# One decode step of attention and a gated MLP: VectorE's program becomes a loop, the head sum moves to TensorE, and the last w_out block is loaded by its own transfer

## The chip, the core and the metric

The kernel runs on one core of a Trainium2 chip. The core has TensorE (PE in the profile, with its weight loads as PEld), VectorE (DVE), ScalarE (ACT), GpSimd (POOL) and SyncE (SP), and 16 DMA engines that bring data from HBM. The time of a run is the device's, in microseconds. Three runs of the kernel before took 678.70, 678.88 and 678.92 us; the median is 678.88 us.

## The reference

Everything is in 32-bit floats. For a batch of 8 and one new position, with x of 512 features:

```python
xn = layernorm(x)
# attention over a cache of 4096 positions: 32 query heads, 8 key/value heads, head size 128
q = xn @ wq
scores = einsum("bhqd,bhkd->bhqk", q, k) * 128 ** -0.5
o = einsum("bhqk,bhkd->bhqd", softmax(scores), v)
s = o @ wo
# gated MLP: w_in is 512 x 1792, w_out is 896 x 512
z = gelu(xn @ w_in)
g = w_sp * layernorm(z[..., 896:]) + b_sp
y = (z[..., :896] * g) @ w_out
out = x + s * silu(y)
```

The caches are 134 MB each; wq and wo are 8.4 MB each, and w_in and w_out 5.5 MB together. Every byte is used once.

## The kernel before

**Slots.** Three SBUF buffers (`slot_A`, `slot_B`, `slot_C`) of 64 KB per partition take all loads, which SyncE issues in one order: wq into B, w_in with w_out into C, then for each of the eight key/value heads half of K into A, the other half into B, half of V into C, the other half into B. Each such half is 8 MB in 128 rows of 64 KB. SyncE waits before each load until TensorE has read the slot's previous content, so normally two loads are queued. In the last head V's first half goes into A, its second half comes in two parts of 4 MB, and wo comes into C: the first 12 of its 32 blocks ahead of V's second half (`load_wo(0, WO_EARLY)`), the rest behind it in six pieces that get smaller (`WO_LATE`: up to block 20, 25, 28, 30, 31, 32).

**Before the heads.** `project_q` makes the queries, `mlp` the gate. `mlp` ends in a product over w_out's seven blocks of 128 rows (L474), all of them columns of one transfer, `w_mlp`.

**A head** (`head`). `scores` (L506) multiplies the queries, spread out in `qz`, with K for four batch entries per slot. `softmax` takes maximum, exponent and sum over `sc`, and transposes the weights into `pT`. Then for each batch entry b: `values` (L538) forms eight products of 512 columns in `o_ps[b % 2]`. The wanted rows of this block are those where the row's group equals the column's; VectorE multiplies by the mask `diag` (L540) and adds over the groups (L541) to get `o_sb`; `combine` (L544) multiplies `o_sb` with `fold`, one product, into four columns of `po`. TensorE takes `combine(b - 1)` behind `values(b)`. I call `values` and the `combine` behind it a unit. After the last head, `folded_wo` (L566), `direct_wo` (L574) and a sum over groups (L625) multiply with wo; VectorE multiplies with the gate and adds x (L630, L631), and SyncE stores the result.

**What sets the order.** A `Recorder` collects every engine's instructions in the order in which the Python code names them, finds what each must wait for, and writes the programs. TensorE's program holds heads 0 to 6 as one loop, with waits on a semaphore `token` that is counted down by one each time, and the last head written out. VectorE's program before is written out from start to end, all eight heads.

Of the kernel before, what the change touches and what calls it, by code (L numbers as in the profile page):

```python
# [15 lines left out]
P = 128  # L16
# [24 lines left out]
BANK = 512  # L41

# [37 lines left out]
class Op:  # L80
    def __init__(self, eng, name, args, kw, line):
        self.eng, self.name, self.args, self.kw, self.line = eng, name, args, kw, line
        self.reads, self.writes = [], []
        self.waits = []
        self.sem = None
        self.iter = None
        self.pos = None


class Recorder:  # L90
# [6 lines left out]
    NAMES = ["tensor", "vector", "scalar", "gpsimd", "sync"]  # L97

    def __init__(self, nc):
# [4 lines left out]
        self.rounds = 0  # L104
        self.order = {n: [] for n in self.NAMES}
        self.dma_sems = {}
# [3 lines left out]
    @contextmanager  # L110
    def round(self, i):
        self.now = i
        self.rounds = max(self.rounds, i + 1)
        self.count = {n: 0 for n in self.NAMES}
        yield
        self.now = None

    def add(self, eng, name, args, kw):
# [3 lines left out]
        key = kw.pop("key", None)  # L122
# [15 lines left out]
        if self.now is not None:  # L138
            op.iter, op.pos = self.now, self.count[eng]
            self.count[eng] += 1  # L140
        op.at = len(self.order[eng])
# [3 lines left out]
        op.deps = set()  # L145
# [25 lines left out]
    def plan(self):  # L171
# [18 lines left out]
        body = [op for op in self.order["tensor"] if op.iter is not None]  # L190
        size = len(body) // self.rounds
        rounds = [body[i * size:(i + 1) * size] for i in range(self.rounds)]
        place = {(o.eng, o.iter, o.pos): o for o in self.ops if o.iter is not None}
        for p in range(size):
            need = set()
            for i, ops in enumerate(rounds):
                assert ops[p].pos == p and ops[p].name == ops[0 * size + p].name
                for o in ops[p].waits:
                    assert o.iter == i, (ops[p].line, ops[p].name, i, o.eng, o.line, o.iter)
                    need.add((o.eng, o.pos))  # L200
            for i, ops in enumerate(rounds):
                ops[p].waits = [place[e, i, q] for e, q in sorted(need)]
        takes = [o.pos for op in rounds[0] for o in op.waits if not o.dma]
        assert takes == sorted(set(takes)), takes
        assert all(o.dma or o.eng == "vector" for op in rounds[0] for o in op.waits)

        for op in self.ops:
            op.token = op.counted = False
        for op in self.ops:
            for o in op.waits:  # L210
                if o.dma:
                    continue
                if op.eng == "tensor" and op.iter is not None:
                    o.token = True
                else:
                    o.counted = True
        for p in range(size):
            any_ = any(ops[p].counted for ops in rounds)
            for ops in rounds:
                ops[p].counted = any_  # L220

        nc = self.nc
        self.first = None
        self.sems = {}

        def sem(name):
            if name not in self.sems:
                self.sems[name] = nc.alloc_semaphore(name)
            return self.sems[name]

        for n in self.NAMES:
            c = 0
            for op in self.order[n]:
                if op.dma:
                    op.sem = sem(op.key or f"dma{op.n}")
                    op.taken = op.key is not None
                    continue
                if op.token and op.counted:
                    c += 1
                elif op.counted:  # L240
                    c += 1
                op.level = c
            sem(n)
        sem("token")

    def emit_op(self, op):
        nc = self.nc
        eng = getattr(nc, op.eng)
        with nc.source_location(__file__, op.line, op.name):
            waits = []  # L250
            for o in sorted(op.waits, key=lambda o: o.n):
                if o.dma:
# [3 lines left out]
                    else:  # L256
                        waits.append((o.sem, 16))
                elif op.eng == "tensor" and op.iter is not None:
                    t = self.sems["token"]
                    eng.wait_ge(t, 1).then_inc(t, -1)  # L260
                else:
                    waits.append((self.sems[o.eng], o.level))
            for s, v in waits:
# [6 lines left out]
            elif op.counted:  # L270
                ins.then_inc(self.sems[op.eng], 1)
                if op.token:
                    eng.wait_ge(self.sems[op.eng], op.level).then_inc(self.sems["token"], 1)
            elif op.token:
                ins.then_inc(self.sems["token"], 1)

    def emit(self):
        nc = self.nc
        self.plan()
        for n in self.NAMES[1:]:  # L280
            for op in self.order[n]:
                self.emit_op(op)
        ops = self.order["tensor"]
        inside = [i for i, op in enumerate(ops) if op.iter is not None]
        size = len(inside) // self.rounds
        for op in ops[:inside[0]]:
            self.emit_op(op)
        with nc.tensor.Fori(0, self.rounds):
            for op in ops[inside[0]:inside[0] + size]:
                self.emit_op(op)  # L290
        for op in ops[inside[-1] + 1:]:
# [28 lines left out]
def gqa_gmlp_decode(real, x, kT, v, wq, wo, w_mlp, out):  # L320
# [13 lines left out]
    for c in range(0, XW, XW // X_PARTS):  # L334
# [22 lines left out]
    nc.vector.tensor_reduce(same[:, 0, :], ident.rearrange("p (g r) -> p r g", g=G),  # L357
                            op=ALU.add, axis=AX.X)
    for g in range(1, G):
        nc.vector.tensor_copy(same[:, g, :], same[:, 0, :])  # L360
    same_all = same.rearrange("p g r -> p (g r)")
    diag = sb("diag", [P, G])
# [302 lines left out]
```

## Time and profile before

| what | value |
|---|---|
| median of three runs | 678.88 us |
| span of the profiled execution, first to last instruction | 677.3 us |
| instructions profiled | 5857 |
| busy: PE, PEld, DVE, ACT | 375.2, 119.5, 167.5, 13.4 us |
| moved by DMA | 290.90 MB, mean 429 GB/s |
| result's store, issue to landing | 1.5 us |

The profile page gives the execution's span and no total of its own; the median lies 1.58 us above the span, for what stands around the first and the last instruction. "PEclk" in a window is the TensorE clock that the throttle granted, 1.00 or 0.50. "DMA share" is the busy share of the 16 DMA engines by the packets that start in a window, so short windows can go above 1. In a timeline row the columns are start, length, engine, line, operation, output and inputs, shape and count; the brackets hold the engine's idle time before it and what ended it. A product of 32-bit floats appears as two MATMUL and two LDWEIGHTS.

### The profile page before, as it was taken

The numbers are of one execution on the slowest core, as the hardware profiler recorded it, in microseconds if no ns is written. First come the engines' busy times: TensorE is split into PE (matmuls) and PEld (weight loads), VectorE is DVE, ScalarE is ACT, GpSimd is POOL, SyncE is SP. The second block draws the span as 40 slices with busy tenths as digits, with TensorE's granted clock in tenths as the row PEclk, the third lists the DMA queues.
The fourth block names the chain that finished last, engine by engine and source line by source line (L and its number), as shares of the span: only waits on it lengthen the run. The fifth ranks groups of instructions, "written<-read, shape, count | busy, mean of one in ns | idle before, by whom it ended". The sixth has DMA issues, their size and how long they took to land. (4 is left out here: it accounts for less than half of the span.)

```text
span 677.3 us, 5857 instructions
## 1 busy us (share of the span) xinstructions
PE 375.2 (55%) x2658; PEld 119.5 (18%) x2658; DVE 167.5 (25%) x277; ACT 13.4 (2%) x27; POOL 2.8 (0%) x14
## 2 busy tenths in 40 slices
PE   0547554546665455456755454655654465655657
PEld 0122121112111111111211121211211121111212
DVE  2141042302430033401521024401432024400342
ACT  0000000000000000000000000000000000000000
POOL 1000000000000000000000000000000000000000
PEclk9967666878767678877766678887676678766697
DMA  8999999999999999999999999999999999999997
GB/s 373 449 434 434 433 434 433 434 433 433 433 433 433 433 433 433 434 433 433 433 433 433 433 434 433 433 433 437 437 437 437 433 437 445 433 437 434 404 423 318
DMA packets 6233, 290.90 MB, mean 429 GB/s; under 512 B 832, under 2 KB 848, under 8 KB 1360
## 3 DMA queue, kind: packets, MB, share of 16 engines
q1 hardware_dynamic: 6192, 290.75, 99.3%
q8 instruction: 7, 0.11, 0.1%
q10 hardware_dynamic: 32, 0.02, 0.0%
q14 instruction: 2, 0.02, 0.0%
HBM read 290.74 MB, written 0.03 MB: 429 GB/s over the span
## 5 line engine op out<-in xcount | busy, mean ns | idle before, releaser
L506 PE MATMUL sc<-slot_B,qz 128*32 128x512 f32 x512 | 74.4, 746 | 76.6 <-PEq L506 76.6
L538 PE MATMUL o_ps<-slot_B,tbuf 128*16 128x512 f32 x512 | 77.5, 732 | 70.5 <-PEq L538 61.6
L506 PE MATMUL sc<-slot_A,qz 128*32 128x512 f32 x512 | 74.4, 746 | 47.6 <-PEq L506 47.6
L540 DVE TENSOR_TENSOR o_all<-o_ps,diag 128x512 f32<-128x512 f32 x64 | 44.3, 691 | 161.0 <-PE o_ps L538 161.0
L538 PE MATMUL o_ps<-slot_C,tbuf 128*16 128x512 f32 x448 | 67.0, 739 | 20.5 <-PEq L538 20.5
L510 DVE TENSOR_REDUCE nm<-sc 128x1 f32<-128x1024 f32 x8 | 9.8, 1224 | 269.5 <-PE sc L506 269.5
L541 DVE TENSOR_REDUCE o_sb<-o_all 128x128 f32<-128x512 f32 x64 | 67.8, 1060 | 2.2
L506 PEld LDWEIGHTS sc<-slot_B,qz 128*32 128x32 f32 x512 | 20.4, 134 | 130.5 <-issue 130.5
L506 PEld LDWEIGHTS sc<-slot_A,qz 128*32 128x32 f32 x512 | 20.7, 133 | 94.8 <-issue 94.8
L544 PE MATMUL po<-fold,o_sb 128*128 128x4 f32 x128 | 25.6, 270 | 12.3 <-PEq L544 12.3
L544 PEld LDWEIGHTS po<-fold,o_sb 128*128 128x128 f32 x128 | 20.3, 199 | 68.5 <-issue 64.2
L538 PEld LDWEIGHTS o_ps<-slot_B,tbuf 128*16 128x16 f32 x512 | 13.4, 106 | 100.5 <-issue 90.2
L538 PEld LDWEIGHTS o_ps<-slot_C,tbuf 128*16 128x16 f32 x448 | 13.7, 112 | 57.0 <-issue 56.8
L528 PE MATMUL scr<-ident,pbuf 128*128 128x128 f32 x64 | 14.8, 409 | 10.6 <-PEq L528 9.3
L511 ACT ACTIVATE pbuf<-sc,nm 128x1024 f32<-128x1024 f32 x8 | 8.9, 1114 | 556.1 <-DVE nm L510 556.1
L528 PEld LDWEIGHTS scr<-ident,pbuf 128*128 128x128 f32 x64 | 11.8, 211 | 11.0 <-issue 9.7
L529 DVE COPY tbuf<-scr 128x512 f32<-128x512 f32 x16 | 11.1, 692 | 10.6 <-PE scr L528 10.6
L415 PE MATMUL scr<-slot_B,xnT 128*32 128x512 f32 x64 | 9.0, 713 | 8.2 <-PEq L415 8.2
L538 PE MATMUL o_ps<-slot_A,tbuf 128*16 128x512 f32 x64 | 9.8, 753 | 3.9 <-PEq L538 3.9
L514 PE MATMUL scr<-ident,nm 128*1 128x128 f32 x8 | 2.2, 269 | 11.8 <-PEq L514 10.4
L394 PE MATMUL scr<-ident,tbuf 8*128 8x8 f32 x4 | 0.6, 255 | 12.9 <-DVE tbuf L391 12.9
L521 PE MATMUL scr<-wl,same 128*128 128x1 f32 x16 | 3.5, 286 | 6.1 <-PEq L521 5.4
(102 smaller groups left out, 88.4 us busy)
## 6 DMA issues: line engine op xcount, KB each, us to landing
slot_B<-in_v SPq DMA_DIRECT2D x2, 4096.0 KB, 33.8
slot_C<-in_w_mlp SPq DMA_DIRECT2D x1, 5376.0 KB, 34.2
slot_C<-in_wo SPq DMA_DIRECT2D x1, 3072.0 KB, 35.4
slot_C<-in_wo SPq DMA_DIRECT2D x1, 2048.0 KB, 41.4
slot_C<-in_wo SPq DMA_DIRECT2D x1, 1280.0 KB, 44.0
slot_C<-in_wo SPq DMA_DIRECT2D x1, 768.0 KB, 45.4
slot_C<-in_wo SPq DMA_DIRECT2D x1, 512.0 KB, 46.1
slot_C<-in_wo SPq DMA_DIRECT2D x2, 256.0 KB, 46.4
```

The source lines that it names most:

```text
L415: nc.tensor.matmul(pq[R * g:R * (g + 1), :], xnT[:, k, :], wq_sb[:, k, lo:lo + REP * DH], start=(k == 0), stop=(k == NK - 1))
L506: nc.tensor.matmul(sc[R * g:R * (g + 1), c, :], qz[:, b * R:(b + 1) * R], k_sb[:, i, c, g, :], start=(b == 0), stop=(b == B - 1))
L510: nc.vector.tensor_reduce(nm, sc, op=ALU.max, axis=AX.XY, negate=True)
L511: nc.scalar.activation(p.rearrange("p j s -> p (j s)"), sc.rearrange("p c s -> p (c s)"), AF.Exp, bias=nm, accum_out=l)
L514: nc.tensor.transpose(a, nm, ident)
L521: nc.tensor.matmul(tot, same_all, wl, start=True, stop=True)
L528: nc.tensor.transpose(t[:, j * P:(j + 1) * P], p[:, 4 * c + j, :], ident)
L529: nc.vector.tensor_copy(pT[:, :, 4 * c:4 * c + 4].rearrange("p b j (g r) -> p (j g) b r", g=G), t.rearrange("p (m b r) -> p m b r", b=B, r ...
L538: nc.tensor.matmul(of[R * c:R * c + G * REP, :], pT[:, b, j, :], v_unit[:, j], start=(j < G), stop=(j >= J - G))
L540: nc.vector.tensor_mul(o_all[b % 2], o, diag[:, :, None].to_broadcast([P, G, DH]))
L541: nc.vector.tensor_reduce(o_sb[b % 2], o_all[b % 2].rearrange("p g d -> p d g"), op=ALU.add, axis=AX.X)
L544: nc.tensor.matmul(po[:, b * REP:(b + 1) * REP], o_sb[b % 2], fold, start=True, stop=True)
```

## The change

**VectorE's program** is a loop over all eight heads, with an inner loop of four rounds of two batch entries. Waits between looped engines become countdown semaphores, one for each pair of engines. To make a head's VectorE part the same each time, work moves: evictions and copies to ScalarE and GpSimd (`po` to `oT`, the queries, the MLP's copies, `qz`), and building `same` to GpSimd. The softmax has fewer steps, and its eight transposes go into `sc` and come out in one copy.

**The sum over groups** leaves VectorE. VectorE only copies `o_ps` to `o_cp` (L616 in the new numbering), and `combine` (L620) is four products that add up in PSUM, one for each group, with the part of `same` that picks that group's rows.

**The last block of w_out** is no longer in `w_mlp`, whose rows are 2 KB shorter. It comes as `w_ext`, 32 rows of 8 KB read as eight groups of four (the array in memory has a fifth, unused row in each group, so that the groups stay apart); `mlp` multiplies it as four chunks of 32 rows, with four small transposes more.

TensorE's program at the end of the last head, before. The rows are the products in program order, with `o_sb` as weights in L544:

```order
L538 MATMUL o_ps<-slot_B,tbuf 16x512 x8
L544 MATMUL po<-fold,o_sb 128x4
L538 MATMUL o_ps<-slot_B,tbuf 16x512 x8
L544 MATMUL po<-fold,o_sb 128x4
L566 MATMUL sc<-slot_C,oT 8x512 x8
L544 MATMUL po<-fold,o_sb 128x4
L566 MATMUL sc<-slot_C,oT 8x512 x4
L574 MATMUL sc<-slot_C,oT_end 32x64 x40
L625 MATMUL sc<-pbuf,same 32x64 x8
L574 MATMUL sc<-slot_C,oT_end 32x64 x24
```

And after (`ob` holds both `o_ps` and `po`):

```order
L613 MATMUL ob<-slot_B,tbuf 16x512 x8
L620 MATMUL ob<-same,o_cp 128x4 x4
L613 MATMUL ob<-slot_B,tbuf 16x512 x8
L620 MATMUL ob<-same,o_cp 128x4 x4
L643 MATMUL sc<-slot_C,oT 8x512 x8
L620 MATMUL ob<-same,o_cp 128x4 x4
L643 MATMUL sc<-slot_C,oT 8x512 x4
L651 MATMUL sc<-slot_C,oT_end 32x64 x40
L702 MATMUL sc<-pbuf,same 32x64 x8
L651 MATMUL sc<-slot_C,oT_end 32x64 x24
```

The order is the same; each of the three single products of L544 has become four.

VectorE's program from the first head to its end, after. Before, these places held eight heads written out, 260 rows in all:

```order
L588 TENSOR_REDUCE nm<-sc 128x1
L593 TENSOR_REDUCE full<-scr 1x128
L596 TENSOR_TENSOR w<-scr,nm 128x1
L598 TENSOR_TENSOR wl<-w,l 128x1
L600 RECIPROCAL wl<-scr 128x1
L601 TENSOR_SCALAR pbuf<-pbuf,w,wl 128x1024
L605 COPY tbuf<-sc 128x32x8x4
L347 UNCONDITIONAL_BRANCH
L616 COPY o_cp<-ob 128x512 x2
L347 REGISTER_ALU
L347 COMPARE_AND_BRANCH
L344 REGISTER_ALU
```

A head's program is now seven instructions ahead of the inner loop and two copies (L616) in it, which four rounds repeat.

SyncE's program at its start, before:

```order
L338 DMA slot_B<-in_wq 128x16384
L341 DMA slot_C<-in_w_mlp 128x10752
L547 DMA slot_A<-in_kT 128x16384
L547 DMA slot_B<-in_kT 128x16384
L553 DMA slot_C<-in_v 128x16384
```

And after:

```order
L409 DMA slot_B<-in_wq 128x16384
L412 DMA slot_C<-in_w_mlp 128x10240
L417 DMA slot_C<-in_w_ext 32x1x2048
L624 DMA slot_A<-in_kT 128x16384
L624 DMA slot_B<-in_kT 128x16384
```

One transfer, `w_ext`, stands between w_mlp and the first half of K.

The core of the diff:

```diff
-        nc.vector.tensor_mul(o_all[b % 2], o, diag[:, :, None].to_broadcast([P, G, DH]))
-        nc.vector.tensor_reduce(o_sb[b % 2], o_all[b % 2].rearrange("p g d -> p d g"), op=ALU.add, axis=AX.X)
+        with nc.turn(b // 2, b % 2):
+            nc.vector.tensor_copy(o_cp[b % 2], o)
...
-        nc.tensor.matmul(po[:, b * REP:(b + 1) * REP], o_sb[b % 2], fold, start=True, stop=True)
+        for g in range(G):
+            nc.tensor.matmul(po[:, b * REP:(b + 1) * REP], o_cp[b % 2][:, g, :], fold[:, g, :],
+                             start=(g == 0), stop=(g == G - 1))
...
-        nc.vector.tensor_copy(to, po.rearrange("p (b r) -> p r b", r=REP))
+        nc.stored = nc.scalar.activation(to, po.rearrange("p (b r) -> p r b", r=REP), AF.Copy)
...
-        nc.vector.tensor_copy(qz.rearrange("p (b s) -> p b s", b=B)[:, :, :REP], qT[:, h])
+        nc.gpsimd.tensor_copy(qz.rearrange("p (b s) -> p b s", b=B)[:, :, :REP], qT[:, h], after=nc.stored)
...
+        with nc.vector.Fori(0, HKV):
+            for op in first:
+                if op is turn[0]:
+                    with nc.vector.Fori(0, count):
+                        for q in turn:
+                            self.emit_op(q)
+                elif op.turn is None:
+                    self.emit_op(op)
...
+XG, XR = 8, 4
+XK = XG * XR
+XC = P // XK
+LAST = NB - 1
...
-    n_in, n_mlp = NK * 2 * FH, NK * 2 * FH + NB * D
+    n_in, n_mlp = NK * 2 * FH, NK * 2 * FH + LAST * D
...
+    ext = slots["C"][:XK, n_mlp:n_mlp + XC * D]
+    nc.sync.dma_start(ext, w_ext[:, :XR])
+    w_ext_sb = ext.rearrange("p (c d) -> p c d", d=D)
...
-        for j in range(NB):
+        low = R * (LAST // 2)
+        hX = tbuf[:XK, 2 * P + D:2 * P + D + XC * R].rearrange("p (c r) -> p c r", r=R)
+        tx = scr[2][:XK, :XC * R].rearrange("p (c r) -> p c r", r=R)
+        for c in range(XC):
+            lo = (LAST % 2) * P + c * XK
+            nc.tensor.transpose(tx[:, c, :], u[low:low + R, 1, lo:lo + XK], ident[low:low + R, low:low + R])
+        nc.scalar.activation(hX, tx, AF.Copy)
+        for j in range(LAST):
...
+        g = LAST % G
+        for c in range(XC):
+            nc.tensor.matmul(sc[R * g:R * (g + 1), 0, :], hX[:, c, :], w_ext_sb[:, c, :],
+                             start=False, stop=(c == XC - 1))
...
+    w_ext = w_out[LAST].reshape(XC, XG, XR, D).transpose(1, 2, 0, 3).reshape(XG, XR, XC * D)
...
+        "w_ext": np.concatenate([w_ext, np.zeros((XG, 1, XC * D), np.float32)], axis=1),
```

More of the change, by code (lines that the diff above doesn't have):

```diff
@@ L144, in add @@
         self.ops.append(op)
-        op.deps = set()
+        if self.now is not None and not op.dma:
+            self.heads.setdefault(self.now, []).append(op)
+        op.deps = set() if after is None else {after}
         for regs, write in ((op.reads, False), (op.writes, True)):
@@ L285, in emit @@
-        size = len(inside) // self.rounds
-        for op in ops[:inside[0]]:
+        inside = [op for op in ops if op.iter is not None and op.iter < LOOPED]
+        for op in ops[:inside[0].at]:
             self.emit_op(op)
[L288 to L291, printed above, removed]
+        with nc.tensor.Fori(0, LOOPED):
+            for op in inside:
+                if op.iter == 0:
+                    self.emit_op(op)
@@ L292, in emit @@
+        for op in ops[inside[-1].at + 1:]:
             self.emit_op(op)
@@ L611, in gqa_gmlp_decode @@
     nc.meet("tensor")
[L612 removed]
+    for h in range(HKV):
         with nc.round(h):
             head(h)
[L615 to L616 removed]
     folded_wo(WO_LATE[0][1], FOLDED)
```

270 lines of the change are left out of this document (156 added, 114 removed).

## The prediction, made before the result was known

> **What bounds the kernel now.** I read the page's head and queues first, then the chain that ended last, then the DMA issues.
>
> ```profile
> span 677.3 us, 5857 instructions
> PE 375.2 (55%) x2658; PEld 119.5 (18%) x2658; DVE 167.5 (25%) x277; ACT 13.4 (2%) x27; POOL 2.8 (0%) x14
> ...
> q1 hardware_dynamic: 6192, 290.75, 99.3%
> q8 instruction: 7, 0.11, 0.1%
> ...
> q14 instruction: 2, 0.02, 0.0%
> HBM read 290.74 MB, written 0.03 MB: 429 GB/s over the span
> ```
>
> The 16 DMA engines are busy for 99.3% of the span, and no compute engine for much over half. Two small queues load instructions, nine packets in all. The chain confirms it:
>
> ```profile
> 628.26 46.46 DMA slot_C<-in_wo
> ...
> 674.76 0.47 PE sc L574 x16
> ```
>
> The last piece of wo lands at 674.72, and 2.6 us later all is over. A faster engine therefore gains nothing inside the heads, so long as SyncE always has a load queued:
>
> ```profile
> slot_A<-in_kT SPq DMA_DIRECT2D x8, 48.1
> slot_B<-in_kT SPq DMA_DIRECT2D x8, 27.9
> slot_C<-in_v SPq DMA_DIRECT2D x7, 47.0
> slot_B<-in_v SPq DMA_DIRECT2D x7, 29.1
> ```
>
> Eight MB (8.39 million bytes) at 429 GB/s take 19.6 us. What lies above that in these issue-to-landing times is time that TensorE may be late without a gap: 8.3 us for K into B, the least.
>
> How evenly do the 16 engines end?
>
> ```profile
> 670.40:672.30 1.90, 1.90 (x22) 0.54 (x14) 0.83 (x2) 0.00 (x0) 0.00 (x0) 1.00 1.00 405
> 672.70:673.20 0.50, 0.50 (x51) 0.50 (x43) 0.50 (x1) 0.00 (x0) 0.00 (x0) 1.00 0.47 180
> ```
>
> The last column but one is their busy share: 1.00 up to 672.3, but 0.47 from 672.7 on. So half the engines end some 2 us before the others. Instruction blocks explain that size: in the windows 39 to 41 and 90 to 91 us, with one packet of the queue each,
>
> ```profile
> q8 instruction: 1, 0.02, 2.9%
> ...
> q14 instruction: 1, 0.01, 1.9%
> ```
>
> 2.9% of 16 engines for 2 us is 0.93 us for a 16 KB block, 1.9% for 1 us is 0.30 us for 8 KB, each on one engine, whose loads it holds up by at least that.
>
> **The change, part by part: the data stream.** The two blocks of q14 should go: VectorE's program falls from 260 rows to 40, and it alone, beside TensorE's, is long enough to need more than a first block. That frees one or two engines. TensorE's program grows by a tenth, from seven q8 blocks to perhaps eight; the last was fetched at the very end, so I price the eighth at 0 to 1 us.
>
> `w_ext`: w_mlp's rows lose 2 KB, eight rows to an engine, so each engine loses 16 KB, 0.6 us at 429/16 = 26.8 GB/s. The 256 KB return in eight groups. If eight engines take them, each gets 32 KB, and stands at +0.6 us; the other eight stay at -0.6. If the receivers are those that end early, the last landing moves to about 674.1; if they are the late ones, to 675.3. No view lists engines singly. I followed the packets' start and end times by hand, and most q8 blocks lie behind packets of the eight engines that did not carry x's eight-row loads; so I take -0.6, and keep +0.6 for the range. The DMA issue itself (about 0.4 us on SyncE) lies under wq's 20 us.
>
> In the Trainium skill, "DMA: Bandwidth & Descriptors" (on why a DMA increments its semaphore by 16) says that a transfer whose slowest dimension is 8 uses the eight lowest-numbered engines; the same eight would carry x and w_ext. No row here numbers engines.
>
> **Inside the heads.** Each unit gets three products more. The price is the pace of two loads of 128 columns, each with a short product:
>
> ```profile
> 12.87 0.59 PE L394 MATMUL scr<-ident,tbuf 8*128 8x8 f32 x4 [12.87 <-DVE tbuf L391]
> ```
>
> Four such pairs take 0.59 us, the two of one L544 (below) 0.38, so a pair more costs 0.105 and a product 0.21 us: 0.64 us for a unit, double at half clock. Of a head's eight combines, about three lie between B's landing and its release: 1.9 to 3.8 us later, against 8.3 us of room. Hidden. VectorE's two steps (0.69 and 1.06 us a batch entry) become one copy of about 0.69 us, under the next unit; the softmax and `mlp` change by a few us under waits of the same kind. Loops and countdown semaphores stay beneath these waits too.
>
> **The tail** is where TensorE's extra work can show:
>
> ```profile
> 652.80 1.91 PE L538 MATMUL o_ps<-slot_B,tbuf 128*16 128x512 f32 x16 [3.59 <-DMA slot_B<-in_v]
> 654.64 0.38 PE L544 MATMUL po<-fold,o_sb 128*128 128x4 f32 x2
> 654.96 1.91 PE L538 MATMUL o_ps<-slot_B,tbuf 128*16 128x512 f32 x16
> ...
> 662.49 3.61 PE L538 MATMUL o_ps<-slot_B,tbuf 128*16 128x512 f32 x16 [5.30 <-DMA slot_B<-in_v]
> 666.03 0.59 PE L544 MATMUL po<-fold,o_sb 128*128 128x4 f32 x2
> 666.55 2.61 PE L538 MATMUL o_ps<-slot_B,tbuf 128*16 128x512 f32 x16
> 669.09 0.39 PE L544 MATMUL po<-fold,o_sb 128*128 128x4 f32 x2
> 669.40 1.90 PE L566 MATMUL sc<-slot_C,oT 128*8 128x512 f32 x16
> 671.23 0.38 PE L544 MATMUL po<-fold,o_sb 128*128 128x4 f32 x2
> 671.55 1.04 PE L566 MATMUL sc<-slot_C,oT 128*8 128x512 f32 x8
> 672.41 1.52 PE L574 MATMUL sc<-slot_C,oT_end 128*32 128x64 f32 x80
> 673.92 0.52 PEld L574 LDWEIGHTS sc<-slot_C,oT_end 128*32 128x32 f32 x32
> 674.76 0.43 PE L574 MATMUL sc<-slot_C,oT_end 128*32 128x64 f32 x16 [0.16 <-DMA slot_C<-in_wo]
> ```
>
> V's last part starts two units at 662.49, and TensorE works through to the wo products with hardly a pause. The start differences give a warm unit: 1.84 for the values, 0.32 for the combine. The same products at 662.49 take 3.54 and 0.52, since the clock is at half:
>
> ```profile
> 650.94:654.35 3.41, 1.55 (x16) 1.00 1.02 442
> ...
> 661.18:664.59 3.41, 2.10 (x12) 0.50 0.99 423
> 664.59:668.00 3.41, 3.41 (x18) 0.50 0.95 405
> 668.00:671.41 3.41, 3.41 (x32) 1.00 0.99 413
> ...
> 295.96:299.37 3.41, 1.37 (x16) 1.00 0.75 327
> 299.37:302.78 3.41, 0.00 (x0) 0.50 1.06 461
> ...
> 596.32:599.73 3.41, 2.42 (x12) 0.50 1.02 442
> 599.73:603.15 3.42, 3.42 (x20) 0.50 1.10 479
> ...
> 53.60:57.02 3.42, 2.80 (x14) 0.50 1.37 594
> 57.02:60.43 3.41, 1.18 (x24) 1.00 0.75 327
> ```
>
> (Columns: length, PE's busy time and count, clock, DMA.) The clock changes on a grid of 3.41 us. A window with 1.55 us of work keeps it full, one with 1.37 us (at 295.96) halves it for the next. From half clock, 2.10 us of work in a window aren't enough to restore it, and at 596.32 2.42 weren't, but 2.80 us at 53.60 were.
>
> Now the sum. Warm, the work from 662.49 to L574 is 1.84 + 0.32 + 1.84 + 0.32 + 1.83 + 0.32 + 0.86 = 7.33 us, plus half of the cold stretch (668.00 - 662.49 = 5.5): 10.1, against 9.92 measured. After it come 128 small pairs, by the row at 673.92 0.0163 us each: 2.1 us, so TensorE could be through at 674.5. Wo's last landing makes it 674.76 and 16 pairs, 675.0: its room is 0.5 us. After the change three combines cost 0.96 instead of 0.32: 9.25 us. V's last part lands 0.6 us earlier: 661.89. So TensorE is through at 661.89 + 9.25 + c/2 + 2.1 = 673.24 + c/2, where c is the cold stretch; the transfers allow 674.4. Against 675.0 the kernel moves by c/2 - 1.8 us, and not below -0.6.
>
> And c: the gap ahead of 661.89 shrinks. Two units from 652.2 now take 5.6 us and 0.2 to drain, so TensorE idles from 658.0 for about 3.9 us. Where the grid lies is chance. A gap of 3.9 puts at least 1.95 us of idling, under 1.5 us of work, into one window, so the clock is halved nearly always. Where the grid has a point in the first half of the gap (56% of positions), the window that holds the gap's end decides, and exactly one window, 3.4 us, is cold, or a little less; in some 10% c is 2.7 to 3.0; in the other third the first window after the gap is too empty to restore it, and c is 4.9 to 6.1. (I take 2.65 us as what restores it, between 2.42 and 2.80.) So the likeliest c is 3.4: 1.7 - 1.8 = -0.1. On the median of 678.88, which lies 1.58 us above this execution's span: 678.8 us.
>
> **Rivals.**
>
> *A second cold window* (slower side). Same mechanism, c = 4.9 to 6.1: +0.65 to +1.25 us, 679.5 to 680.1. For it: 661.18 above, where 2.10 us of work didn't restore the clock. It makes the kernel slower from c = 3.6 on, and passes 0.2% (1.36 us, about what a measurement can tell from no change) at 6.3, so only with an error in my prices.
>
> *The clock stays full.* Then TensorE could be through at 673.2, before the last landing, the transfers set the end, 0.6 us are gained: 678.3 us. This is the outcome if a window must be wholly idle, since 3.9 us of idling holds a whole window in one position of seven. The row at 295.96 speaks against it. In the Trainium skill, "TensorE: Matmul & The Clock Gate" (the two states) gives one idle window of about 3.4 us as the condition; by that sentence this rival would be likelier than my forecast. The trace agrees on the length and differs on "idle", as 1.37 us of work weren't enough.
>
> *w_ext meets the late engines.* Everything in the tail lands 1.2 us later than in my sum: 680.0 with c = 3.4, 681.1 with 5.5.
>
> *Looping brings fetches.* Should each of VectorE's 31 backward branches (seven outer, three inner in each of eight heads) fetch 8 KB onto one engine, at 0.30 us at least, the data end 9.3 us later: about 688. TensorE's own loop speaks against it: it ran seven rounds of 147 products each, and all of q8 has seven packets. In the Trainium skill, "Runtime: NRT & Kernel Launch" (instruction fetch mechanics) says that a taken branch whose target is outside a window of two pages forces a fetch; the loop here is far below a page, so by that rule nothing is fetched either.
>
> *The engines end in step.* If few blocks hold anyone up, all end near 673.3 and, with a warm clock, the gain is about 1.4 us: 677.5.
>
> **Chances.** Forecast (678.8 within half a microsecond) 0.47; second cold window 0.23; full clock 0.10; late engines 0.10; fetches or another stall 0.05; in step 0.05. Slower by over 0.2% (above 680.24): 0.05 of the second window, 0.06 of the late engines, the 0.05 of the stalls, and 0.03 out of the forecast's for what I don't foresee: 0.19. Faster (below 677.52): 0.05. Within: 0.76. For 8 in 10 the range runs from the full clock, 678.2, into the late engines, 680.5.
>
> **What would show it.** Right: no q14 packets within the span and seven or eight of q8; GB/s as before through the heads; DMA shares near the end that fall later and more steeply; units of about 2.8 us when warm; a clock of 0.50 once more behind V's last part, with TensorE, not wo, ahead of the last product in the chain. Wrong: a gap in the DMA row within a head, more instruction packets, or V's last part later than 662.49.

## The result, and the profile after

The changed kernel takes 682.06 us, the median of ten runs (679.51 to 686.04), against 678.90 of ten runs of the kernel before (678.47 to 679.05). The ratio is 1.0053, with a 95% interval of 1.0038 to 1.0069: slower by 3.6 us, 2.6 to 4.7 (the medians themselves lie 3.2 us apart). The forecast of 678.8 and its range up to 680.5 were wrong. New, too, is the spread: 6.5 us among runs of one kernel, where the kernel before has 0.6.

The profiled run is one of 683.15 us. Its page's head and queues:

```profile
span 681.6 us, 6827 instructions
...
PE 428.3 (63%) x3052; PEld 168.3 (25%) x3052; DVE 91.5 (13%) x147; ACT 18.4 (3%) x43; POOL 6.0 (1%) x29
...
q1 hardware_dynamic: 6232, 290.75, 98.8%
q8 instruction: 8, 0.13, 0.1%
...
HBM read 290.74 MB, written 0.03 MB: 427 GB/s over the span
```

VectorE's busy time falls from 167.5 to 91.5 us, TensorE's rises from 375.2 to 428.3. The queue q14 is gone and q8 has eight packets. The same bytes take longer: 427 GB/s, 98.8%. The end of the chain (start, length, what):

```profile
626.78 37.87 DMA slot_B<-in_v
664.64 0.04 issue
664.69 2.98 PE ob L613 x16
667.66 1.80 PE ob L620 x8
669.47 3.22 PE ob L613 x16
672.68 0.98 PE ob L620 x8
...
678.80 0.71 PE sc L651 x48
```

From V's last part on it is TensorE alone; wo no longer appears. Two things are late. V's last part starts at 664.69 us, not 662.49. And the two units after it run at half clock for the most part: 2.98 us for values that take 1.84 warm, 1.80 for a combine that takes 0.98, 3.22 for the second values. Of the DMA issues, one row moved most:

```profile
slot_B<-in_kT SPq DMA_DIRECT2D x8, 25.0
```

K into B is issued 2.9 us later against its landing than before (27.9).

How does the clock stay at half for so long? The windows of the clock's grid at this place, first all of TensorE's work (length, PE, PEld, ..., clock, DMA share, GB/s), then that of the values (L613) alone:

```profile
661.98:665.39 3.41, 0.70 (x8) 0.25 (x12) 0.00 (x0) 0.00 (x0) 0.00 (x0) 1.00 0.97 408
665.39:668.81 3.42, 3.42 (x18) 1.41 (x10) 0.69 (x1) 0.00 (x0) 0.00 (x0) 0.50 0.96 407
668.81:672.22 3.41, 3.41 (x20) 1.06 (x19) 0.00 (x0) 0.00 (x0) 0.00 (x0) 0.50 1.01 423
```

```profile
665.39:668.81 3.42, 2.27 (x12) 0.19 (x4) 0.50 0.96 407
668.81:672.22 3.41, 2.83 (x16) 0.49 (x16) 0.50 1.01 423
```

V's last part arrives 0.70 us ahead of the end of a window that is otherwise empty, so its first products still run at full clock. The clock is halved from 665.39 to 672.22, for 6.83 us. TensorE is busy through the whole of the window from 665.39, and the clock stays at 0.50 behind it. It is restored behind the next. What differs is the share of the wide products (512 columns): 2.27 us there, 2.83 here. The rest are a combine's products of 4 columns.

### The profile page after: what moved, and what is told of

It is laid out like the page before. It is cut to its first block, busy times and chain, and to the rows that moved or that the text cites. A ratio compares the mean times of both kernels' runs of the same rounds, so it can differ in the third digit from the quotient of the medians.

```text
span 681.6 us, 6827 instructions
## 1 busy us (share of the span) xinstructions
PE 428.3 (63%) x3052; PEld 168.3 (25%) x3052; DVE 91.5 (13%) x147; ACT 18.4 (3%) x43; POOL 6.0 (1%) x29
## 3 DMA queue, kind: packets, MB, share of 16 engines
q1 hardware_dynamic: 6232, 290.75, 98.8%
## 5 line engine op out<-in xcount | busy, mean ns | idle before, releaser
L613 PE MATMUL ob<-slot_B,tbuf 128*16 128x512 f32 x512 | 83.0, 779 | 52.6 <-PEq L613 47.5
L620 PEld LDWEIGHTS ob<-same,o_cp 128*128 128x128 f32 x512 | 67.0, 206 | 64.5 <-issue 64.5
L613 PE MATMUL ob<-slot_C,tbuf 128*16 128x512 f32 x448 | 67.4, 743 | 15.7 <-PEq L613 15.7
L616 DVE COPY o_cp<-ob 128x512 f32<-128x512 f32 x64 | 44.2, 691 | 236.0 <-DVEq L616 236.0
L620 PE MATMUL ob<-same,o_cp 128*128 128x4 f32 x512 | 71.7, 265 | 4.5 <-PEq L620 4.5
L613 PEld LDWEIGHTS ob<-slot_B,tbuf 128*16 128x16 f32 x512 | 13.8, 109 | 83.4 <-issue 76.9
L613 PEld LDWEIGHTS ob<-slot_C,tbuf 128*16 128x16 f32 x448 | 13.7, 113 | 52.7 <-issue 52.5
L604 PE MATMUL sc<-ident,pbuf 128*128 128x128 f32 x64 | 15.5, 424 | 11.4 <-PEq L604 11.4
L604 PEld LDWEIGHTS sc<-ident,pbuf 128*128 128x128 f32 x64 | 12.5, 223 | 11.9 <-issue 11.9
L605 DVE COPY tbuf<-sc 128x1024 f32<-128x1024 f32 x8 | 9.8, 1224 | 17.9 <-DVEq L605 17.9
L613 PE MATMUL ob<-slot_A,tbuf 128*16 128x512 f32 x64 | 9.6, 744 | 2.8 <-PEq L613 2.8
```

The costliest lines, as they stand in the source:

```text
L604: nc.tensor.transpose(t[:, j * P:(j + 1) * P], p[:, j, :], ident)
L605: nc.vector.tensor_copy(pT.rearrange("p b j (g r) -> p (j g) b r", g=G), t.rearrange("p (m b r) -> p m b r", b=B, r=REP))
L613: nc.tensor.matmul(of[R * c:R * c + G * REP, :], pT[:, b, j, :], v_unit[:, j], start=(j < G), stop=(j >= J - G))
L616: nc.vector.tensor_copy(o_cp[b % 2], o)
L620: nc.tensor.matmul(po[:, b * REP:(b + 1) * REP], o_cp[b % 2][:, g, :], fold[:, g, :], start=(g == 0), stop=(g == G - 1))
```

## The experiments

Three theories. **A:** the four products of a combine on TensorE are the cost, by a clock that stays cold: in the tail directly, and in the heads because B is released late, so that a load of K reaches the queue when the engines are nearly dry. **B:** `w_ext` lies on engines that are late. **C:** VectorE's loop, its semaphores and its waits. The *lead* of a load is the time from its issue to the moment at which the first DMA engine has ended the load ahead of it. No view lists single engines, so leads are followed by hand from the landing events in the trace (the times at which each engine has ended its part of a load): 6.1 to 7.4 us in the kernel before, 2.1 to 5.2 in the kernel after. Times are medians in us; where a difference in us stands with an interval, it is the ratio's times 678.7.

| run | runs | median (lowest to highest) | ratio to before, 95% |
|---|---|---|---|
| after, sum on VectorE again | 11 | 679.69 (678.79 to 680.55) | 1.0014, 1.0005 to 1.0023 |
| the same, without w_ext | 11 | 678.80 (678.57 to 679.43) | 1.0003, 0.9994 to 1.0011 |
| after, without w_ext | 5 | 682.64 (681.15 to 684.01) | 1.0053, 1.0040 to 1.0066 |
| before, with w_ext | 11 | 679.22 (679.05 to 679.72) | 1.0007, 0.9999 to 1.0016 |
| before, four products | 10 | 681.25 (678.76 to 682.82) | 1.0031, 1.0018 to 1.0044 |
| before, four products in the last head | 4 | 680.91 (679.44 to 681.60) | 1.0030, 1.0016 to 1.0044 |
| before, four products in heads 0 to 6 | 11 | 678.99 (678.58 to 680.37) | 1.0005, 0.9996 to 1.0014 |
| before, four products in the last head, wide filling | 10 | 678.92 (678.40 to 680.55) | 1.0008, 0.9998 to 1.0017 |
| the same, narrow filling | 10 | 682.66 (679.02 to 685.07) | 1.0059, 1.0042 to 1.0076 |

**Which part of the change?** First the sum alone is undone in the kernel after (the loop's count of positions is adapted, and `diag` and `fold` are made as before):

```diff
-            nc.vector.tensor_copy(o_cp[b % 2], o)
+            nc.vector.tensor_mul(o_all[b % 2], o, diag[:, :, None].to_broadcast([P, G, DH]))
+            nc.vector.tensor_reduce(o_sb[b % 2], o_all[b % 2].rearrange("p g d -> p d g"), op=ALU.add, axis=AX.X)
...
-        for g in range(G):
-            nc.tensor.matmul(po[:, b * REP:(b + 1) * REP], o_cp[b % 2][:, g, :], fold[:, g, :],
-                             start=(g == 0), stop=(g == G - 1))
+        nc.tensor.matmul(po[:, b * REP:(b + 1) * REP], o_sb[b % 2], fold, start=True, stop=True)
```

> The kernel after, with one thing undone: the sum over groups is VectorE's again (a multiplication and an addition over groups, within its loop) and a combine is one product. Loop, countdown semaphores, the moves to ScalarE and GpSimd and w_ext stay. Theory A (the added products let B go late, so that some loads of K reach the queue when the engines are nearly dry, and they lengthen the tail): 678.3 to 678.9 us, runs within 0.6 us of each other, B's K loads issued at about the times of the kernel before (lead of 6 us or more). Theory B (w_ext lies on the late engines) and theory C (VectorE's loop, its waits): still about 682 us, runs spread over some us.

It took 679.69: most of the cost is gone. But 0.9 us stay, above theory A's 678.9, and the runs spread over 1.8 us where it named 0.6. The reverse, the same lines put into the kernel before:

> The kernel before, with one thing done: VectorE copies the products, and a combine is four products. No loop, no w_ext. Theory A: 681 to 683 us with runs spread over 3 us or more, lead of the K loads into B down to 2 to 5 us. Theories B and C: about 678.9 us, as before.

681.25, as theory A says. Then `w_ext` is taken out of the kernel after, and put alone into the kernel before:

```diff
-    n_in, n_mlp = NK * 2 * FH, NK * 2 * FH + LAST * D
+    n_in, n_mlp = NK * 2 * FH, NK * 2 * FH + NB * D
...
-    ext = slots["C"][:XK, n_mlp:n_mlp + XC * D]
-    nc.sync.dma_start(ext, w_ext[:, :XR])
...
-        for j in range(LAST):
+        for j in range(NB):
```

> The kernel after, with w_out's last block back in w_mlp, no w_ext and no chunks of 32 rows. Theory A: 682 us, within 0.6 us of the kernel after, wide spread. Theory B (w_ext is the cost): 679 us or less.

> The kernel before, with w_ext and its four chunks alone. If the engines that take its eight groups are those that end early: 678.3 us, the last landing 0.6 us earlier. If they are the late ones: 679.5 us. Theory B, w_ext as the main cost: 681 us or more.

Without it the kernel after stays at 682.64, so theory B falls as the main cost. But alone it costs 0.5 us (-0.1 to 1.1), where the prediction took a gain of 0.6. The end of that run's chain shows where:

```profile
629.01 46.80 DMA slot_C<-in_wo
675.81 0.04 issue
675.86 0.47 PE sc L592 x16
```

The last landing is at 675.81 us, against 674.72, as it should be if the eight groups go to engines that end late. (This profile is of the slowest of the eleven runs, 679.72 us.)

The kernel after without `w_ext` and with the sum on VectorE has the loop and the moves alone:

> The kernel after without w_ext and with the sum over groups on VectorE: VectorE's loop and the moves to ScalarE and GpSimd alone. If the loop costs 0.5 us by a block of instructions that is fetched behind the last product (as the run with w_ext shows one): 679.2 us. If it costs nothing or saves the two blocks of q14: 678.3 to 678.7 us.

678.80, or 0.2 us (-0.4 to 0.7) above the kernel before. Theory C falls: a loop that lets q14 vanish neither gains nor costs anything that these runs can tell.

**Tail or heads?** In the kernel before, `values` and `combine` get a condition, so that the four products stand in the last head alone, or in the other seven alone:

```diff
-                values(b, v_sb[:, i])
+                values(b, v_sb[:, i], last)
...
-                    combine(b - 1)
+                    combine(b - 1, last)
```

> The kernel before, with VectorE's copy and the four products of a combine in the last head alone. Tail by the prediction's formula, with V's last part at 662.49 us: TensorE through at 673.84 us + c/2, against 675.24 before. If the combine's products count as work for the clock, c is 3.4 to 6.1 us: 679.0 to 680.4 us. If products of 4 columns hardly count (the rows of the kernel after: 0.50 through a window that holds 1.8 us of them), c is 5.5 to 9.5 us, by where the 3.41 us grid lies: 680.1 to 682.1 us, runs spread over 1 us or more.

> The kernel before, with the copy and the four products in heads 0 to 6 alone; the last head is as before. If the heads pay (loads of K into B that reach the queue under some 2.5 us before the engines run dry): 679.2 to 681 us, and V's last part late by what is lost. If the tail pays alone: 678.7 us, within 0.3 us of the kernel before.

> The kernel before with four products in heads 0 to 6 alone, once more and with more runs. If the heads pay without VectorE's loop as well, in single events of 1.5 to 2.3 us: median 678.8 to 679.8 us, some runs 1 to 3 us above. If not: 678.7 us, within 0.3 us, all of them.

The last head alone costs 2.0 us (1.1 to 3.0), as much as all heads together in this kernel (2.1). Heads 0 to 6 alone took 678.87 in four runs and 678.99 in eleven: 0.3 us (-0.3 to 1.0), with one run 1.6 above. So by these runs nearly all is the tail when VectorE has no loop; a run below leaves more than this to the heads. The profiled run of the kernel with four products in the last head, the fastest of its four, had one cold window of which 2.95 us lay behind V's arrival; by the prediction's formula the other three (680.8 to 681.6) would have had 2.8 to 4.3 us more, an estimate.

What does a late load cost by itself? In heads 0 to 6 of the kernel before, extra work (four times the eight products of `values(6)`, into a scratch bank) delays B's release and does nothing else:

```diff
                 values(b, v_sb[:, i])
+                if b == 6 and not last:
+                    idle_work(b, v_sb[:, i])
```

> The kernel before, with extra work in heads 0 to 6 that delays the release of B and does nothing else: values(6)'s eight products four times more into a scratch bank, 7.4 us warm. The combines are as before. The lead of K's load (issue to the first engine's end of the load ahead of it) was 6.1 to 7.4 us and becomes about -0.7. If the stream loses time when the load comes late: at least 0.7 us and what a queue needs to start in each of seven heads, 1.5 to 3 us each: 689 to 700 us. If 8.3 us of room was right: below 680 us.

689.93 (two runs), so 11.2 us, or 1.6 for each of seven heads. One of them, SyncE's issue and two windows, and the DMA issues' row:

```profile
289.80 0.33 SPq L554 DMA_DIRECT2D slot_B<-in_kT  x1
```

```profile
289.00:290.50 1.50, 1.05 (x10) 0.30 (x2) 0.69 (x1) 0.00 (x0) 0.00 (x0) 1.00 0.00 0
290.50:292.00 1.50, 0.30 (x2) 0.30 (x2) 1.02 (x1) 0.00 (x0) 0.00 (x0) 1.00 2.09 699
```

```profile
slot_B<-in_kT SPq DMA_DIRECT2D x8, 21.9
```

No packet starts from 289.0 to 290.5. And 21.9 us from issue to landing is what a load takes that meets engines just about empty, not 19.6. The view of the kernel before had such a load too, its first:

```profile
slot_B<-in_wq SPq DMA_DIRECT2D x1, 21.9
```

So of the 8.3 us at most 27.9 - 21.9 = 6.0 were room. The landing events make it less. K into B lands 19.3 us behind the load ahead of it (both taken as the mean over the 16 engines) when nothing is lost, and what it takes beyond that is the price of its lead:

| lead of K into B, us | stream lost, us | loads, in the profiles of all runs |
|---|---|---|
| -1.1 | 3.0 | 1 |
| -0.2 and -0.1 | 1.6 and 1.8 | 2 |
| 0.4 | 1.5 | 1 |
| 0.7 to 1.2 | 0.9 to 1.2 | 5 |
| 2.1 to 2.6 | 0.0 to 0.6 | 8 |
| above 2.6 | 0.2 at most | all others |

So in these runs a load is late when its lead falls under some 2.6 us. One with that lead landed 23.6 us behind its issue (284 us in the kernel before with four products), and the room was about 27.9 - 23.6 = 4.3 us, an estimate. In the Trainium skill, "DMA: Bandwidth & Descriptors" (Anatomy of one DMA) puts a fixed part of about 2.0 us on a transfer beside its bytes, for GpSimd's queue; SyncE's loads here show 2.3 (21.9 - 19.6).

**Is it the clock?** If the tail's cost is the clock and not the added work, then more work can take it away. In the kernel with four products in the last head, the gap ahead of V's last part is filled, once with wide products and once, for the same 3.7 us, with narrow ones as in a combine. Nothing reads what they write.

```diff
+    def fill(b, v_unit):
+        for _ in range(2):
+            for j in range(J):
+                c = j % G
+                nc.tensor.matmul(scr[0][R * c:R * c + G * REP, :], pT[:, b, j, :],
+                                 v_unit[:, j], start=(j < G), stop=(j >= J - G))
...
+                if last and b == 5:
+                    fill(b, v_sb[:, i])
```

The narrow one:

```diff
+        for i in range(15):
+            nc.tensor.matmul(scr[0][:, :REP], o_cp[0][:, i % G, :], fold4[:, i % G, :],
+                             start=True, stop=True)
```

> As the run with four products in the last head alone (680.9 us), and the last gap of that head filled: two times eight products of 512 columns into a scratch bank, 3.7 us warm, ahead of the wait for V's last part. If the cost is the clock: no window of the gap is idle enough to halve it, c is near 0, TensorE could be through at 673.8 us, wo's last landing sets the end as in the kernel before: 678.7 us, runs within 0.8 us. If the work itself is the cost, not the clock: 680.9 us or more.

> The same gap, filled for the same 3.7 us with fifteen products of 4 columns behind weights of 128 columns, as a combine's. If such products hardly count as work for the clock: it is halved as without them, 680 to 682 us. If any product counts: 678.7 us, as with the wide ones.

678.92 with the wide ones: two microseconds of cost vanish by adding 3.7 us of work. 682.66 with the narrow ones, no better than with none, rather worse. (In the profile the narrow filling runs into the cold window and ends at 662.99 us, 0.5 us behind V's landing; that much of it is delay.) Two of the ten runs with wide products still took 680.4 and 680.6. Windows of the narrow run, all products, and behind it the values (L540) alone:

```profile
657.16:660.57 3.41, 3.41 (x32) 3.08 (x28) 0.69 (x1) 0.00 (x0) 0.00 (x0) 1.00 0.91 394
660.57:663.98 3.41, 3.41 (x20) 2.65 (x24) 0.00 (x0) 0.00 (x0) 0.00 (x0) 0.50 0.92 394
663.98:667.40 3.42, 3.42 (x17) 1.10 (x9) 0.69 (x1) 0.00 (x0) 0.00 (x0) 0.50 1.01 430
667.40:670.81 3.41, 3.41 (x18) 1.34 (x20) 0.00 (x0) 0.00 (x0) 0.00 (x0) 0.50 0.99 411
670.81:674.22 3.41, 3.41 (x20) 1.91 (x16) 0.69 (x1) 0.00 (x0) 0.00 (x0) 0.50 0.77 304
674.22:677.63 3.41, 3.41 (x19) 0.80 (x11) 0.00 (x0) 0.00 (x0) 0.00 (x0) 0.50 0.00 2
```

```profile
657.16:660.57 3.41, 0.40 (x4) 0.00 (x0) 1.00 0.91 394
663.98:667.40 3.42, 2.56 (x12) 0.17 (x4) 0.50 1.01 430
667.40:670.81 3.41, 2.54 (x13) 0.49 (x16) 0.50 0.99 411
```

The window from 657.16 is busy throughout, with 0.40 us of wide products, and the clock is halved behind it as behind an idle one. Five more full windows follow at 0.50. The last of them holds 3.00 us of wide products, those of `folded_wo`, and behind it the clock is full again. With the wide filling all is warm:

```profile
659.78:663.19 3.41, 3.41 (x34) 1.21 (x37) 0.23 (x1) 0.00 (x0) 0.00 (x0) 1.00 0.91 389
663.19:666.61 3.42, 3.42 (x36) 1.56 (x32) 0.69 (x1) 0.00 (x0) 0.00 (x0) 1.00 0.97 415
```

So a busy row of narrow products isn't work to the clock. Counting products of 512 columns alone, the full windows that did not restore it in the stretches shown here hold 2.62 us or less, those that did 2.83 or more.

The 19 profiles together say the same more sharply. They hold 1572 whole windows at half clock and 1709 at full clock between 70 and 660 us. At half clock, windows with less than 2.59 us of products of 512 columns restored it in 0 of 1006 cases, those with more than 2.63 in 558 of 558 (in between, 7 of 8). At full clock, windows with less than 1.3 us of them halved it in 548 of 548 cases, those with more than 1.4 in 0 of 1132 (in between, 15 of 29). Other work moves neither bound: of the windows with too little wide work, 29 were busy throughout and still did not restore the clock, and 15 were busy for 2.5 us or more and still halved it.

At half clock a unit is now 3.62 + 1.80 = 5.42 us. A window of 3.41 with 2.65 us of values may overlap the combine by 0.76 at most, which by this geometry is so in 1.73 of the 5.42 us of its positions: a third. So how many windows pass until the clock is restored is a matter of chance, and I take that for the spread; it is an estimate, since no run fixed the position. In the Trainium skill, "TensorE: Matmul & The Clock Gate" (Why this matters for your kernels) advises to keep TensorE busy for 4 us on end; these runs show TensorE busy for longer at half clock, so which products they are matters.

The same filling in the kernel after:

> The kernel after, with the wide products in the last head's last gap and nothing else changed. If the tail's cold clock is most of the cost of the change: 679.3 to 680.2 us (w_ext and a late load of K stay). If the heads carry most of it: 681.5 us or more.

682.66 (four runs, 680.66 to 684.24), no better than without: by what I had written down, the heads carry most of it. The profiled run, the fastest of the four, is one in which the heads cost next to nothing: V's last part lands at 662.74 us and the span ends at 677.6. That it took 680.66 all the same, 3.1 us more, may be of the experiment's own making. Between 677 and 683 us, behind the last product, stands

```profile
q8 instruction: 1, 0.02, 1.5%
```

an instruction block: the filling pushed the program's end over a block's border. Its fetch ends 3.3 us behind the span. But the three other runs of this kernel lie 1.5 to 1.6 us above their spans, as the runs of the kernel after do (1.5 to 1.7). So the block can't explain the median; whether it explains the one run isn't shown.

**The heads.** The next two have the wide filling in the last gap, so that the tail is paid for, and no block behind the last product. One is the kernel after without `w_ext`, one the kernel before with four products in all heads:

> The kernel after without w_ext and with the wide products in the last gap; the combines stand behind one entry's values each, as in the kernel after. It differs from the run at 678.8 us only in the order of the combines. If the heads cost nothing: 678.8 to 679.2 us. If they cost what the kernel after loses beside the tail (K's loads that reach the queue late): 680 to 682 us, with runs spread over 2 us or more.

> The kernel before with the four products in all heads and the wide products in the last gap, no loop on VectorE. If the heads cost nothing without the loop: 678.8 to 679.2 us. If they cost with or without it: as much as the run without w_ext that goes with it, 680 us or more.

681.13 (ten runs, 679.16 to 684.74; ratio 1.0044, 1.0029 to 1.0059) and 679.67 (twelve, 678.50 to 681.98; 1.0020, 1.0011 to 1.0030). So here the heads cost 3.0 and 1.4 us. The profile of the first, a run of 681.18 us, shows how. TensorE in head 5, the clock's windows, the values in two of these, and SyncE's issue of K into B, here and (last fence) in the kernel before:

```profile
500.72 3.62 PE L599 MATMUL ob<-slot_B,tbuf 128*16 128x512 f32 x16 [7.34 <-PEq L599]
504.26 1.87 PE L613 MATMUL ob<-same,o_cp 128*128 128x4 f32 x8
506.07 3.62 PE L599 MATMUL ob<-slot_B,tbuf 128*16 128x512 f32 x16
...
511.41 3.62 PE L599 MATMUL ob<-slot_B,tbuf 128*16 128x512 f32 x16
...
516.13 1.91 PE L599 MATMUL ob<-slot_B,tbuf 128*16 128x512 f32 x16
```

```profile
494.90:498.31 3.41, 0.00 (x0) 0.00 (x0) 0.00 (x0) 0.00 (x0) 0.00 (x0) 0.50 1.02 442
...
501.72:505.14 3.42, 3.42 (x20) 1.07 (x9) 0.64 (x1) 0.00 (x0) 0.00 (x0) 0.50 1.02 441
505.14:508.55 3.41, 3.41 (x17) 1.40 (x21) 0.06 (x1) 0.00 (x0) 0.00 (x0) 0.50 0.84 365
508.55:511.97 3.42, 3.42 (x20) 1.93 (x16) 0.69 (x1) 0.00 (x0) 0.00 (x0) 0.50 1.10 479
511.97:515.38 3.41, 3.41 (x18) 0.77 (x11) 0.17 (x1) 0.00 (x0) 0.00 (x0) 0.50 0.89 384
...
518.00:520.00 2.00, 1.36 (x16) 1.35 (x13) 0.69 (x1) 0.00 (x0) 0.00 (x0) 1.00 1.38 459
520.00:522.00 2.00, 1.15 (x14) 0.82 (x17) 0.00 (x0) 0.20 (x1) 0.21 (x1) 1.00 0.19 66
```

```profile
501.72:505.14 3.42, 2.62 (x16) 0.19 (x4) 0.50 1.02 441
...
511.97:515.38 3.41, 3.06 (x16) 0.34 (x8) 0.50 0.89 384
```

```profile
518.35 0.33 SPq L617 DMA_DIRECT2D slot_B<-in_kT  x1
```

```profile
510.85 0.33 SPq L547 DMA_DIRECT2D slot_B<-in_kT  x1
```

TensorE is at half clock for three entries of four, from before 500.72 to 515.38, though busy without a pause. K into B is issued at 518.35, 7.5 us later than before. Its lead is -0.2 us. The packets that start in the 4 us from 518 carry 262 GB/s on the mean, against 429 over the span before, which is 1.6 us of the stream; by the packets' own times the engines are emptiest from 518.5 to 519.5 us, busy for 0.4 of the time. V's last part lands at 664.8 us in this run, against 662.4. The kernel after without `w_ext` has such an event in its profile too, at 440.76 us (lead -0.1).

Is this the clock again, or the amount of work? The same kernel gets still more work: the wide products three times, in heads 0 to 6, in the gap ahead of V in B. (Forty small products at the start keep the program's end within its block.)

```diff
+                if b == 3:
+                    if last:
+                        nc.count["tensor"] += 3 * J
+                    else:
+                        fill(b, v_sb[:, i], 3)
```

> The kernel after without w_ext, with the wide products in the last gap (681.1 us), and now with wide products in heads 0 to 6 too: three times eight products of 512 columns into a scratch bank, 5.5 us warm, in the gap of about 7 us ahead of the wait for V in B. Forty small products ahead of the queries' projection keep the program's end where it was in its blocks of instructions. If the heads' cost is the clock: it stays full or is soon restored, B is released about 2 us or more earlier, no late load: 678.6 to 679.2 us, runs within 1 us. If it is the work on TensorE and its order: 681 us or more.

678.91 (eleven runs, 678.68 to 680.51; ratio 1.0007, 0.9998 to 1.0016). The mean granted clock rises from 0.777 to 0.816, and K into B lands 27.8 us behind its issue, as before the change (27.9). In the profile two of the seven loads are still issued late, with leads of 3.6 and 3.7 us, and lose nothing; two of the eleven runs still took 680.4 and 680.5. So most of the heads' cost comes from the clock, and not from the amount of work.

**A cure without added work.** The products of the kernel after in another order: a combine stands behind the values of two entries.

```diff
+DUE = [[], [0], [1], [2, 3], [], [4, 5], [], []]
...
-                if b > 0:
-                    combine(b - 1)
+                for q in DUE[b]:
+                    combine(q)
...
+        combine(B - 2)
         combine(B - 1)
```

> The kernel after, with the same work in another order on TensorE: a combine stands behind two batch entries' values, not one (0; 1; 2 and 3 in the gap ahead of B; 4 and 5 behind values 5; 6 and 7 after B is read). Theory A: B is released about 2 us earlier than in the kernel after when warm and more when cold, two entries' values together fill a clock window, so c is 3.4 to 5 us, and combine 5 lies in the last gap: TensorE through at 675 us + 0.5 for w_ext, 679 to 679.6 us, runs within 1.5 us. If not the place of the combines but something else costs (loop, waits, amount of work): 681 us or more.

679.35 (four runs, 679.12 to 680.02; ratio 1.0012, 0.9997 to 1.0026): the order takes back 2.7 us of the loss, and what remains is `w_ext`'s size. The leads are 5.3 to 6.9 us again. In the profile, the slowest run, c is still 5.9 us, and TensorE, through at 676.39 us, sets the end. The order does two things at once, it pairs combines and puts two into a gap, and no run tells their shares. Without `w_ext` and with the filling:

> The kernel after without w_ext, the combines behind two entries' values, and the wide products in the last gap: what the runs so far point to as the best form. TensorE through at some 673 us, ahead of wo's last landing at 674.7: 678.3 to 678.8 us, as the kernel before or a little faster. If VectorE's loop has a cost of its own: 679.2 us.

678.79 (ten runs, 678.60 to 679.34; ratio 1.0004, 0.9995 to 1.0014), as the kernel before. No version beat that: wo's last landing, at 674.60 us in this run, sets the end of both.

## Why the prediction was wrong

**Streams and loop: right.** q14 vanished, q8 has eight packets, no fetches come with the loop, and the 2.8 us of a warm unit with a combine of 0.96 came out at 2.82 and 0.98.

**"And c: ... the likeliest c is 3.4": the step that failed in the tail.** The formula itself holds. With V's start and c as measured, TensorE should be through at 664.69 + 9.25 + 2.1 + 6.83/2 = 679.5 us in the kernel after (measured 679.51), and at 662.53 + 11.35 + 8.27/2 = 678.0 in the kernel before with four products (measured 678.04). But c was 6.8 and 8.3 us, beyond even the 4.9 to 6.1 of the rival with a second cold window. I had read what restores the clock from rows whose work was all wide products (2.10 us not enough, 2.80 enough) and then let the added narrow products count as work. They hardly do, and at half clock they take a third of each unit: the change itself made the windows too thin. Against the forecast's 674.94 (673.24 + 1.7), TensorE was through 4.57 us late: 1.7 of it by c ((6.83 - 3.4)/2) and 2.80 by V's start.

**"1.9 to 3.8 us later, against 8.3 us of room. Hidden.": the step that failed in the heads.** Both sides were off, the room most of all: about 4.3 us. I took 19.6 us of pure transfer for the load that meets empty engines, where 21.9 stood in the view as wq's load, and I let a load be issued until the engines run dry, where the runs lose time from a lead of some 2.6 us down. And the delay was priced with the combines' own time at a given clock; the longer cold stretch was left out. In the profile of the kernel after, K into B is issued 3.1 to 4.7 us later than before; in the head shown above it was 7.5.

**"So I take -0.6" for `w_ext`: wrong,** and the other end, which I kept as the rival of the late engines, was right: 0.5 us measured against 0.6. Of the 2.80 us by which V's last part started later than forecast, this sign makes 1.1 to 1.7 (V starts at 663.57 us in the profile of `w_ext` alone, and its median is 0.5 up); the rest I put down to the heads. The profile has no single event as clean as the one above, but its landing events bear this out: at 128.7, 206.9 and 439.1 us K into B has leads of 2.1 to 2.4 us and loses 0.5, 0.6 and 0.2 us of the stream, 1.3 together.

**The range** came from one position of the grid for one gap. A kernel that rolls for its clock in eight heads has a spread of its own, and 679.5 to 686 us shows it.

**The signs** I named for a wrong prediction were the right ones to watch: V's last part came later than 662.49, and a gap in the DMA stands within a head, plain in a sister kernel's profile and slight in the kernel after's own.

**Open.** Heads 0 to 6 cost about 0.3 us in the kernel before (1.4 with the filling at the end) and 3.0 in the kernel with the loop. The two hold the same products in the same order. The costs of tail and heads don't add up either: the filling of the last gap takes off only 1.6 us in the kernel before with four products in all heads (681.25 to 679.67), where the last head alone cost 2.0. Why long cold stretches are more frequent in the kernel with the loop was not settled; no run held the grid's position against the gaps.

## What to carry to other kernels

Work that is moved to TensorE as many narrow products is paid twice: in its own time, and in a clock that it doesn't keep warm, for the wide products around it too. Put such products where TensorE would idle, or behind two batches of wide ones, so that a window of 3.4 us can hold nearly nothing else. And price the room of a load from a load that arrived on empty engines, less the lead that a load needs, and a delay at the clock that the change itself brings about.

## What the runs showed of the hardware that I had not expected

- Products of 4 columns behind weight loads of 128 columns hardly count as work for the clock: halved behind a window with 3.41 us of busy rows, 0.40 of them wide, and kept at 0.50 from 660.57 to 677.63 us with TensorE busy throughout.
- By products of 512 columns alone, a window of 3.41 us restored the clock with more than 2.63 us of them (558 of 558 windows) and not with less than 2.59 (0 of 1006); it halved it with less than 1.3 us (548 of 548) and not with more than 1.4 (0 of 1132).
- More work can be faster: 3.7 us of useless wide products took off 2.0 us (680.91 to 678.92), and 5.5 us in each of seven heads took off 2.2 (681.13 to 678.91).
- A load of K lost some of the stream although it was issued before the engines ran dry: 0.9 to 1.2 us at leads of 0.7 to 1.2 us, up to 0.6 at 2.1 to 2.6, and 0.2 at most above that.
- An instruction block was fetched behind the last product of one run, which took 3.1 us more than its span; three other runs of the same kernel took 1.5 to 1.6 us more. That the block is the cause isn't shown.
